# A second Strassen level over pairs of column blocks in the gate/up stage of a gated FNet and GeGLU mix

## The chip, the cores and the metric

One core of one Trainium2 chip runs one program. The metric is the device time of that program in microseconds, as the median of several runs. A profiled execution of the kernel before and its trace are at hand. Engines: PE (TensorE, matmuls), PEld (its weight loads), DVE (VectorE), ACT (ScalarE), POOL (GpSimd, which here only issues stores), SP (SyncE, which only issues loads).

## The reference

For x of 2048 tokens by 640 channels, in float32, the kernel computes

```
g = sigmoid(sum(x * gate_w))                      # one value per token
a = Re(DFT over tokens(DFT over channels(x)))     # four DFT matrices given as inputs
b = (gelu(x @ w_gate) * (x @ w_up)) @ w_down      # w_gate, w_up: 640 x 1728, w_down: 1728 x 640
out = g * a + (1 - g) * b
```

The part that changes is `x @ w_gate` and `x @ w_up`. `gate_w` enters only through g, which is called the gate logit before its sigmoid.

## The kernel before, in words

**Products.** Every float32 product is done in three matmuls (`mm3`, lines 85 to 87): each operand is split into a rounded high part (ACT, `high`, L74) and the rest as low part (DVE, `low`, L77), and high x high, high x low and low x high are added in one PSUM bank. All three have a 128 x 128 weight tile and 512 moving columns.

**Strassen, first level.** Tokens come in four tiles of 512, as two token pairs (`tp` 0 and 1); x is transposed, so that tokens are columns. The 640 channels are five inner blocks of 128. A weight block f holds 128 columns of w_gate and 128 of w_up, so that with two tokens of a pair there is a 2 x 2 block product. Four of the five inner blocks go in two twos, written W[name, i] for i = 0, 1, and are multiplied by Winograd's form of Strassen's scheme with seven products (A11, S1, S2, A12, S3, S4, A22 against B11, T1, T2, B21, T3, B22, T4); the fifth inner block is multiplied plainly (`g5`, `u5` and their difference `D`) and added into the same banks. One block costs 54 matmuls per token pair.

**Order.** The program has five stages one behind the other: a first block of columns (`first_products`), the gate/up stage (`gate_up`, f from 1 to 12), the down product (`split_k`, `step_k`), the Fourier stage over tokens (`cseq`, 64 steps with operands split two steps ahead) and the last product over channels, with the mixing. In the gate/up stage the two token pairs are recorded alternately, step by step, and the order of the instructions on each engine is left to the framework's scheduler; elsewhere `in_order` (L92) fixes the recorded order of the engines that it names. Buffers in SBUF come from pools: `slot` (L64, 48 buffers of 4 KB per partition) for nearly all large tiles, `mtile` (12 of 2 KB), `wsmall` (4 of 1 KB). PSUM has eight banks. A tile's first writer waits until the former owner of its buffer is done.

**Around the change.**

- `load_w` (L186) loads the weights of block f + 1, makes the sums S1 to S4 on DVE and splits both.
- `gate_up` (L259): bank X takes A11, is copied to `s1` (L131), takes S2 on top, is copied to `s2`, then S3 and A22; bank Z takes S1 and `u5`, is copied to `s5` (L277), then S4 and D; bank V takes A12 and `g5`, added to `s1` (L284). Gelu on `s1` (L285) and `s2` (L293). Products and their differences are stored by POOL to DRAM as hA and hT (`keep`, L235), for the down stage.
- After every block come, on DVE, the sums of w_down's (`sum_wd`) or, for the last stage, of the Fourier matrices' blocks (`sum_wu`, L333), each stored in one DMA by `sums_left` (L316).
- `load_z` (L369) loads 128 tokens of x, multiplies by gate_w (L373) and reduces (L374); sixteen times in the stage. `gate_rows` (L350) takes the sigmoid, transposes it on PE (L354) and stores it, after block 10.

Of the kernel before, what the change touches and what calls it, by code (L numbers as in the profile page):

```python
# [1 line left out]

# [22 lines left out]
GM_AT = [2, 15]  # L25
EORD = [0, 2, 1, 3, 4]


@with_exitstack
def kernel(  # L30
# [33 lines left out]
    def slot(dt, shape, name):  # L64
        return pool.tile(shape, dt, tag="s4", name=name, bufs=48)

# [6 lines left out]
    def high(hi, raw):  # L73
        nc.scalar.activation(hi, raw, AF.Copy)  # L74
# [32 lines left out]
    z = pool.tile([P, NS], F32, tag="z", name="z")  # L107
    gwb = slot(F32, [P, D], "gwb")

# [9 lines left out]
    def pair(dt, name):  # L119
        return slot(dt, [P, 2, T], name)  # L120
# [62 lines left out]
    def wsmall(dt, name):  # L183
        return pool.tile([P, 2, P], dt, tag="w", name=name, bufs=4)

    def load_w(f):  # L186
        ra, *a = wchunk(f"wa{f}")
        rb, d = wsmall(F32, f"wb{f}"), wsmall(F32R, f"wd{f}")
        nc.sync.dma_start(ra, wf[f - 1, :, :8])
        nc.sync.dma_start(rb, wf[f - 1, :, 8:])  # L190
        sm, *c = wchunk(f"ws{f}")
        g01, g23, u23 = ra[:, 0:2], ra[:, 2:4], ra[:, 5:7]
        high(a[0], ra)
        tt(sm[:, 0:2], rb, u23, op=ALU.add)
        tt(sm[:, 4:6], g01, rb, op=ALU.subtract)
        tt(sm[:, 2:4], sm[:, 0:2], g01, op=ALU.subtract)
        tt(sm[:, 6:8], g23, sm[:, 2:4], op=ALU.subtract)
        high(c[0], sm)
        low(*a, ra)
        tt(rb[:, 1], ra[:, 4], ra[:, 7], op=ALU.subtract)  # L200
        high(d[:, 0], rb[:, 1])
        low(*c, sm)
        low(d[:, 0], d[:, 1], rb[:, 1])
        W = {"D": (d[:, 0], d[:, 1])}
        for i in range(2):
            W["A11", i], W["A12", i], W["A22", i] = at(a, i), at(a, 2 + i), at(a, 5 + i)
            for k in range(4):
                W[f"S{k + 1}", i] = at(c, 2 * k + i)
        W["g5"], W["u5"] = at(a, 4), at(a, 7)
        return W  # L210

# [44 lines left out]

    hid = {}

    def gate_up(f, W, B, tp, s5):  # L259

        n = f"{f}_{tp}"
        X, Z, V = bank(f"pX{n}"), bank(f"pZ{n}"), bank(f"pV{n}")
# [11 lines left out]
        mm3(Z, W["u5"], x2, False, True)  # L276
        nc.scalar.activation(s5, Z, AF.Copy)  # L277
        yield
        prod(X, "S2", "T2", False)
        s2 = copy(X, f"s2{n}")  # L280
        yield
        prod(V, "A12", (2, 1), True)
        mm3(V, W["g5"], x1, False, True)
        tt(s1, s1, V, op=ALU.add)  # L284
        nc.scalar.activation(s1, s1, AF.Gelu_apprx_tanh)  # L285
        yield
        prod(X, "S3", "T3", False)
        tt(s5, s5, X, op=ALU.add)
        yield
        prod(Z, "S4", (2, 2), False)  # L290
        mm3(Z, W["D"], x2, False, True)
        tt(s2, s2, Z, op=ALU.add)  # L292
        nc.scalar.activation(s2, s2, AF.Gelu_apprx_tanh)  # L293
        tt(s2, s2, s5, op=ALU.mult)  # L294
        keep(hA[tp][k], 1 + 2 * second, s2)
        if second:
            h12, t1 = hid.pop(tp)
            tt(h12, s2, h12, op=ALU.subtract)
# [3 lines left out]
        yield  # L302
        prod(X, "A22", "T4", False)
        mm3(X, W["u5"], x1, False, True)
        tt(s1, s1, X, op=ALU.mult)
        keep(hA[tp][k], 2 * second, s1)
        if second:
            tt(s5, s1, t1, op=ALU.subtract)
            keep(hT[tp][k], 3, s5)
        else:  # L310
            tt(s5, s2, s1, op=ALU.subtract)
            keep(hT[tp][k], 0, s5)
            hid[tp] = s2, s5
        yield

    def sums_left(n, r, a21, to):  # L316

        sm = slot(F32, [P, 8, P], f"{n}s")
        a11, a12, a22 = r[:, 0:2], r[:, 2:4], r[:, 6:8]
        tt(sm[:, 0:2], a21, a22, op=ALU.add)  # L320
        tt(sm[:, 4:6], a11, a21, op=ALU.subtract)
        tt(sm[:, 2:4], sm[:, 0:2], a11, op=ALU.subtract)
        tt(sm[:, 6:8], a12, sm[:, 2:4], op=ALU.subtract)
        nc.gpsimd.dma_start(to, sm)

    def sum_wd(k):

        r, a21 = slot(F32, [P, 8, P], f"dr{k}"), wsmall(F32, f"da{k}")
        nc.sync.dma_start(r, wd[k, :, :8])
        nc.sync.dma_start(a21, wd[k, :, 8:])  # L330
        sums_left(f"d{k}", r, a21, wsd[k])

    def sum_wu(p):  # L333


        r, a21 = slot(F32, [P, 8, P], f"ur{p}"), wsmall(F32, f"ua{p}")
        nc.sync.dma_start(r, wu[p, :, :8])
        nc.sync.dma_start(a21, wu[p, :, 8:])
        if p > 1:
            v, r = r, slot(F32, [P, 8, P], f"un{p}")  # L340
            for a, b in ((0, 2), (2, 4), (4, 5), (5, 8)):
                kept = p == 4 and a in (0, 4)
                nc.scalar.activation(r[:, a:b], v[:, a:b], AF.Copy, scale=1.0 if kept else -1.0)
            if p < 4:
                v, a21 = a21, wsmall(F32, f"ub{p}")
                nc.scalar.activation(a21, v, AF.Copy, scale=-1.0)
            nc.gpsimd.dma_start(wneg[p], r)
        sums_left(f"u{p}", r, a21, wsu[p])

# [18 lines left out]

    def load_z(sb):  # L369

        r = slot(F32, [P, D], f"xz{sb}")
        nc.sync.dma_start(r, xz[sb])
        nc.vector.tensor_tensor(r, r, gwb, op=ALU.mult)  # L373
        nc.vector.tensor_reduce(z[:, sb : sb + 1], r, axis=mybir.AxisListType.X, op=ALU.add)  # L374

# [62 lines left out]
    def load_k(i):  # L438


        tp, b, k = kseq[i]
        n = f"{tp}{b}{k}"
        if k == NK and b:
            return
        r = slot(F32, [P, 8, P], f"kw{n}")
        if k == NK:
            m = slot(F32, [P, 8, P], f"km{n}")
            nc.sync.dma_start(r[:, :5], wd0)
            for q in range(2):
                nc.sync.dma_start(m[q * FR : (q + 1) * FR, :5], wdr)  # L450
            r, src = (r, m), h0[tp]
        elif b:
            nc.sync.dma_start(r[:, 0:2], wd[k, :, 6:8])
            nc.sync.dma_start(r[:, 2:8], wsd[k][:, 0:6])
            src = hT[tp][k]
        else:
            nc.sync.dma_start(r[:, 0:6], wd[k, :, 0:6])
            nc.sync.dma_start(r[:, 6:8], wsd[k][:, 6:8])
            src = hA[tp][k]
        raw = []  # L460
        for q in range(2):
            raw.append(pair(F32, f"kr{n}{q}"))
            nc.sync.dma_start(raw[q], src[:, 2 * q : 2 * q + 2])
        kraw[i] = r, raw

    def split_k(i):
# [160 lines left out]
    with in_order(ACT, DVE, PE):  # L627
# [60 lines left out]
        first_out(bk1, 1, 1)  # L688
        W = load_w(1)
# [4 lines left out]
        tsum(3)  # L694
        his("T1", "T3")
        first_out(bk2, 1, 2)
        lows("T1")
        tsum(2)
        lows("T3")
        his("T2")  # L700
        tsum(4)
        his("T4")
        lows("T2", "T4")
    loads.close()
    Bs.append(B)
    zq = list(range(NS))
    for f in range(1, NF):
        nxt = load_w(f + 1) if f + 1 < NF else None
        s5 = pair(F32, f"s5{f}")
        work = [gate_up(f, W, Bs[tp], tp, s5[:, tp]) for tp in range(2)]  # L710
        for step in range(7):
            for w in work:
                next(w)
            if f == NF - 1 and step >= 4:
                load_k(step - 4)
                if step == 6:
                    split_k(0)
        if f % 2:
            sum_wd(f // 2)
        elif f <= 2 * ND:  # L720
            sum_wu(f // 2 - 1)
        if f == NF - 3:
            gate_rows()
        for _ in range(2):
            if f > 1 and zq:
                load_z(zq.pop(0))
        W = nxt
    order = ctx.enter_context(ExitStack())
# [66 lines left out]
    X = Z = V = L = Q = R = Y = None  # L795
    sv = {}
    for i, (j, ri, b, sp) in enumerate(cseq):
# [321 lines left out]
```

## Time and profile before

| | us |
|---|---|
| median of 3 runs | 1030.67 |
| lowest and highest | 1030.64, 1030.9 |
| the profiled execution | 1030.49 |
| its span, first to last instruction | 1028.7 |

The profile's views tell of one execution, with times in us from the first instruction. A row of a group gives line, engine, operation, what is written and read, the number of instructions, then the busy time of all, the mean of one in ns, and the idle time ahead of them with what ended it. A row of the timeline gives start, duration and the instruction. Matmuls overlap, so the distance between starts says more than their durations. The gate/up stage lies at about 46 to 341 us, the down stage behind it until about 511, the Fourier stage until about 903.

### The profile page before, as it was taken

How to read it: one execution, taken by the hardware profiler on the slowest of the kernel's cores; microseconds unless marked ns; L12 is line 12 of the kernel's file. 1: busy time of each engine (PE TensorE's matmuls, PEld its weight loads, DVE VectorE, ACT ScalarE, POOL GpSimd, SP SyncE). 2: the span in 40 equal slices, each digit the busy share in tenths (PEclk: the TensorE clock that was granted, in tenths of full speed). 3: DMA queues.
4: the chain of work that ended last, by engine and by line, in shares of the span. 5: the costliest groups of instructions: out<-in, count | busy, mean ns of one | idle time of the engine just before them, and what ended most of it. 6: DMA issues, size and time to landing. Idle time of an engine off the chain costs nothing.

```text
span 1028.7 us, 12846 instructions
## 1 busy us (share of the span) xinstructions
PE 1024.4 (100%) x4540; PEld 846.7 (82%) x4540; DVE 774.7 (75%) x1048; ACT 451.7 (44%) x579; POOL 132.1 (13%) x237
## 2 busy tenths in 40 slices
PE   9999999999999999999999999999999999999998
PEld 7888888888888888888888888888888888888887
DVE  6987676767653967985898975796678769697794
ACT  5553333343523646655445443343344344365340
POOL 0112121212121200100010011002000200021121
PEclk9999999999999999999999999999999999999999
DMA  7346554746475978968766667557756777896855
GB/s 268 112 155 227 208 180 148 248 155 234 154 253 202 310 272 276 318 228 290 273 206 234 209 226 277 182 194 246 255 180 215 281 268 277 301 340 205 272 130 90
DMA packets 78929, 234.05 MB, mean 228 GB/s; under 512 B 10160, under 2 KB 18896, under 8 KB 78864
## 3 DMA queue, kind: packets, MB, share of 16 engines
q1 hardware_dynamic: 58144, 169.31, 48.8%
q0 software_dynamic: 20432, 63.73, 18.0%
q8 instruction: 35, 0.57, 0.2%
q14 instruction: 30, 0.25, 0.1%
q10 hardware_dynamic: 288, 0.20, 0.1%
HBM read 169.21 MB, written 63.98 MB: 227 GB/s over the span
## 4 chain that ended last, share of the span: by engine, by line
PE 99%; DMA 0%; DVE 0%; SPq 0%; ACT 0%; issue 0%
PE pX L87 8%; PE pX L85 8%; PE pX L86 8%; PE pZ L87 5%; PE pZ L85 5%; PE pZ L86 5%; PE pV L86 3%; PE pV L85 3%; PE pV L87 3%; PE pL L87 3%; PE pL L85 3%; PE pL L86 3%; PE pY L87 1%; PE pR L87 1%; PE pQ L87 1%; PE pY L86 1%
## 5 line engine op out<-in xcount | busy, mean ns | idle before, releaser
L74 ACT ACTIVATE ch<-csa 128x1024 fp32r<-128x1024 f32 x32 | 34.0, 1062 | 88.1 <-DVE csa L419 53.1
L131 ACT ACTIVATE s<-pX 128x512 f32<-128x512 f32 x64 | 37.8, 595 | 75.5 <-PE pX L87 70.6
L74 ACT ACTIVATE ch<-cra 128x1024 fp32r<-128x1024 f32 x32 | 33.8, 1057 | 46.0 <-PE pL L86 21.6
L77 DVE TENSOR_TENSOR cl<-crb,ch 128x1024 fp32r<-128x1024 f32 x32 | 39.1, 1221 | 17.2 <-ACT ch L74 9.9
L284 DVE TENSOR_TENSOR s<-s,pV 128x512 f32<-128x512 f32 x24 | 16.4, 684 | 44.8 <-PE pV L87 36.7
L77 DVE TENSOR_TENSOR cl<-cra,ch 128x1024 fp32r<-128x1024 f32 x32 | 39.1, 1222 | 14.3 <-ACT ch L74 14.0
L86 PE MATMUL pL<-cl,xah 128*128 128x512 f32 x128 | 49.8, 389 | 0.0
L87 PE MATMUL pL<-ch,xal 128*128 128x512 f32 x128 | 49.8, 389 | 0.0
L235 POOL DMA_DIRECT2D hA<-s x48 | 26.0, 542 | 183.2 <-DVE s L294 175.6
L85 PE MATMUL pL<-ch,xah 128*128 128x512 f32 x128 | 49.3, 389 | 0.0
L77 DVE TENSOR_TENSOR cl<-csb,ch 128x1024 fp32r<-128x1024 f32 x32 | 39.1, 1223 | 6.6 <-ACT ch L74 5.1
L74 ACT ACTIVATE ch<-crb 128x1024 fp32r<-128x1024 f32 x32 | 33.8, 1055 | 21.1 <-DVE cl L77 7.8
L77 DVE TENSOR_TENSOR cl<-csa,ch 128x1024 fp32r<-128x1024 f32 x32 | 39.1, 1221 | 4.0 <-ACT ch L74 3.3
L77 DVE TENSOR_TENSOR kl<-kw,kh 128x1024 fp32r<-128x1024 f32 (+1 forms) x26 | 31.4, 1208 | 11.1 <-ACT kh L74 11.1
L74 ACT ACTIVATE ch<-csb 128x1024 fp32r<-128x1024 f32 x32 | 33.9, 1059 | 12.1 <-PE pL L86 6.9
L293 ACT ACTIVATE s<-s 128x512 f32<-128x512 f32 x24 | 15.2, 633 | 37.7 <-DVE s L292 37.7
L285 ACT ACTIVATE s<-s 128x512 f32<-128x512 f32 x24 | 15.1, 630 | 32.1 <-DVE s L284 32.1
L793 POOL DMA_DIRECT2D uA<-s x16 | 8.7, 542 | 160.0 <-DVE s L839 153.3
L74 ACT ACTIVATE kh<-kw 128x1024 fp32r<-128x1024 f32 (+1 forms) x26 | 27.1, 1041 | 3.8 <-issue 3.5
L86 PEld LDWEIGHTS pL<-cl,xah 128*128 128x128 f32 x128 | 24.0, 188 | 5.0
L87 PEld LDWEIGHTS pL<-ch,xal 128*128 128x128 f32 x128 | 24.0, 188 | 5.0
L85 PEld LDWEIGHTS pL<-ch,xah 128*128 128x128 f32 x128 | 24.0, 188 | 5.0
(3579 smaller groups left out, 3352.5 us busy)
## 6 DMA issues: line engine op xcount, KB each, us to landing
cra<-in_ct SPq DMA_DIRECT2D x64, 512.0 KB, 4.0
crb<-in_ct SPq DMA_DIRECT2D x64, 512.0 KB, 4.8
hA<-s POOLq DMA_DIRECT2D x48, 256.0 KB, 4.7
hT<-s POOLq DMA_DIRECT2D x48, 256.0 KB, 5.6
kr<-hA SPq DMA_DIRECT2D x24, 512.0 KB, 6.3
kr<-hT SPq DMA_DIRECT2D x24, 512.0 KB, 6.9
ux<-uA SPq DMA_DIRECT2D x24, 512.0 KB, 6.1
ux<-uT SPq DMA_DIRECT2D x16, 512.0 KB, 6.7
```

What stands on the lines that cost most here:

```text
L74: nc.scalar.activation(hi, raw, AF.Copy)
L77: nc.vector.tensor_tensor(lo, raw, hi.bitcast(F32), op=ALU.subtract)
L85: nc.tensor.matmul(ps, lh, rh, start=first, stop=False, skip_group_check=True)
L86: nc.tensor.matmul(ps, lh, rl, start=False, stop=False, skip_group_check=True)
L87: nc.tensor.matmul(ps, ll, rh, start=False, stop=last, skip_group_check=True)
L131: nc.scalar.activation(m, src, AF.Copy)
L235: nc.gpsimd.dma_start(to[:, i], src)
L284: tt(s1, s1, V, op=ALU.add)
L285: nc.scalar.activation(s1, s1, AF.Gelu_apprx_tanh)
L293: nc.scalar.activation(s2, s2, AF.Gelu_apprx_tanh)
L793: nc.gpsimd.dma_start(to[:, i], src)
```

## The change

Blocks 3 to 12 are taken as five pairs. In a pair, the product A12 B21 is computed once for both blocks and both token pairs by a second Strassen level: its 2 x 2 block matrices are A12's two inner blocks of the two column blocks, against the two inner blocks of B21 of the two token pairs. `together` computes its seven products (11 `mm3` with the fifth inner block's) into three banks H, Z, V and leaves the sums in `s1t`; `gate_up` then adds its A11 product to `s1t`, or has it added, instead of copying it, and has no bank V for paired blocks. The sums of x across the token pairs are made once, in block 2 (`sums_across`); the combinations of A12 in `make_w` (`across`), from a third load `rq`.

In the stage PE, ACT and DVE keep the recorded order. Work that prepares other blocks is put into a list (`fills`) and recorded between the steps in proportion to matmul time (`fill`, `run`). Loads of weights are two blocks ahead.

The gate logit is one DVE instruction with an accumulator, and a second that reads it out. `gate_rows` comes after block 12. The `sum_wu` pieces move to Fourier steps 4, 17, 19, 21 and 36 and the two behind each; `sums_left` works in place and stores in four DMAs. The slot pool has 47 buffers, `wsmall` 6, and `gwb` its own.

```diff
+PAIRED = 3
+WU_AT = [4, 17, 19, 21, 36]
...
     def slot(dt, shape, name):
-        return pool.tile(shape, dt, tag="s4", name=name, bufs=48)
+        return pool.tile(shape, dt, tag="s4", name=name, bufs=47)
...
-    gwb = slot(F32, [P, D], "gwb")
+    gwb = pool.tile([P, D], F32, tag="gwb", name="gwb")
...
-        return pool.tile([P, 2, P], dt, tag="w", name=name, bufs=4)
+        return pool.tile([P, 2, P], dt, tag="w", name=name, bufs=6)
+
+    def pair_of(f):
+        return 0 if f < PAIRED or f >= NF else 2 - (f - PAIRED + 1) % 2
...
+        def across():
+            tt(rq[:, 3], rq[:, 0], rq[:, 1], op=ALU.add)
+            tt(rq[:, 5], ra[:, 0], rq[:, 0], op=ALU.subtract)
+            tt(rq[:, 4], rq[:, 3], ra[:, 0], op=ALU.subtract)
+
+        def across2():
+            tt(rq[:, 6], ra[:, 1], rq[:, 4], op=ALU.subtract)
+            tt(rq[:, 7], g5, rq[:, 2], op=ALU.subtract)
...
+        if kind == 1:
+            work = [(84, sums), (84, across), (56, across2), (0, high_q), (84, sums2), (0, high_a), (56, diff)]
+            work += [(109, low_q), (0, high_c), (122, low_a), (122, low_c)]
+        elif kind == 2:
+            work = [(84, sums), (28, diff_here), (0, high_a), (84, sums2), (0, high_c), (97, low_a), (122, low_c)]
+        else:
+            work = [(84, sums), (0, high_a), (84, sums2), (0, high_c), (122, low_a), (56, diff), (122, low_c)]
+        return W, work
...
+    def together(f, W, Tp, s1, xs):
+        H, Z, V = (bank(f"p{name}{f}t") for name in "HZV")
+        x1 = [at(Bs[tp][5], 0) for tp in range(2)]
+        mm3(H, W["A12", 0], Tp["B11"], True, True)
+        yield 68
+        s1[0, 0] = copy(H, f"s1{f}00")
+        yield
+        mm3(Z, W["S1p"], Tp["T1"], True, False)
+        mm3(Z, W["g5n"], x1[1], False, True)
+        yield 136
+        s1[1, 1] = copy(Z, f"s1{f}11")
+        yield
+        mm3(V, W["A12", 1], Tp["B21"], True, False)
+        mm3(V, W["g5"], x1[0], False, True)
+        yield 136
+        tt(s1[0, 0], s1[0, 0], V, op=ALU.add)
+        yield
+        mm3(H, W["S2p"], Tp["T2"], False, True)
+        yield 68
+        s1[0, 1] = copy(H, f"s1{f}01")
+        yield
+        mm3(H, W["S3p"], Tp["T3"], False, True)
+        yield 68
+        tt(s1[1, 1], s1[1, 1], H, op=ALU.add)
+        yield
+        mm3(Z, W["S4p"], Tp["B22"], False, False)
+        mm3(Z, W["Dp"], x1[1], False, True)
+        yield 136
+        tt(s1[0, 1], s1[0, 1], Z, op=ALU.add)
+        tt(s1[0, 1], s1[0, 1], xs[1], op=ALU.add)
+        yield
+        mm3(H, W["A22p"], Tp["T4"], False, False)
+        mm3(H, W["g5n"], x1[0], False, True)
+        yield 136
+        s1[1, 0] = copy(H, f"s1{f}10")
+        yield
...
         prod(X, "A11", (1, 1), True)
-        s1 = copy(X, f"s1{n}")
+        yield 136
+        if not kind:
+            s1 = copy(X, f"s1{n}")
+        else:
+            s1 = s1t[kind - 1, tp] if (kind, tp) != (1, 1) else None
+            if s1 is not None:
+                tt(s1, s1, X, op=ALU.add)
...
+        todo.extend([(122, last_sums), (61, last_sum)])
...
-        nc.gpsimd.dma_start(to, sm)
+            for i, v in enumerate((a22, a11, a21, a12)):
+                nc.gpsimd.dma_start(to[:, 2 * i : 2 * i + 2], v)
...
-        nc.vector.tensor_tensor(r, r, gwb, op=ALU.mult)
-        nc.vector.tensor_reduce(z[:, sb : sb + 1], r, axis=mybir.AxisListType.X, op=ALU.add)
+            nc.vector.tensor_tensor_reduce(v, v, gwb, 1.0, 0.0, ALU.mult, ALU.add, z[:, sb : sb + 1])
...
+    def fill(ns):
+        state["pe"] += ns
+        some = False
+        while fills and not (some and not fills[0][0]) and state["done"] <= 1.25 * state["all"] * state["pe"] / state["pe_all"]:
+            cost, do = fills.popleft()
+            do()
+            some = True
+            state["done"] += cost
...
+    with in_order(PE, ACT, DVE):
+        for f in range(1, NF):
...
+            work = [gate_up(f, W, Bs[tp], tp, s5[:, tp], s1t, xs) for tp in range(2)]
+            more = together(f, W, Tp, s1t, xs) if kind == 1 else iter(())
+            for _ in range(4):
+                run(more)
+            for step in range(8 if not kind else 7):
+                for tp, w in enumerate(work):
+                    run(w)
+                    if (step, tp) in ((0, 1), (1, 0)):
+                        run(more)
+                        if step == 0:
+                            run(more)
+                if step == 5:
+                    load_w(f + 2)
...
+            if f == NF - 1:
+                gate_rows()
...
+        for p, at_i in enumerate(WU_AT):
+            if i == at_i:
+                wus[p] = sum_wu(p)
+            if at_i <= i < at_i + 3:
+                next(wus[p], None)
```

More of the change, by code (lines that the diff above doesn't have):

```diff
@@ L1 @@
+from collections import deque
 from contextlib import ExitStack, contextmanager
+from functools import partial
 import concourse.bass as bass
@@ L201, in load_w @@
[L201 to L206, printed above, removed]
-            for k in range(4):
-                W[f"S{k + 1}", i] = at(c, 2 * k + i)
-        W["g5"], W["u5"] = at(a, 4), at(a, 7)
-        return W
+        rq = None
+        if pair_of(f) == 1:
+            rq = slot(F32, [P, 8, P], f"wq{f}r")
+            nc.sync.dma_start(rq[:, 0:3], wf[f, :, 0:3])
@@ L255, in first_out, with gate_up @@
         keep(h0[tp], t - 1, g)
[L257 to L259 removed]
+    hid, todo = {}, deque()
+    def together(f, W, Tp, s1, xs):
[34 more added lines that the diff above has]
+        yield
+    def gate_up(f, W, B, tp, s5, s1t, xs):
         n = f"{f}_{tp}"
[L264 removed]
+        kind = pair_of(f)
+        X, Z = bank(f"pX{n}"), bank(f"pZ{n}")
+        xs[tp] = X
         x1, x2 = at(B[5], 0), at(B[5], 1)
@@ L272, in gate_up @@
         prod(X, "A11", (1, 1), True)
-        s1 = copy(X, f"s1{n}")
-        yield
+        yield 136
+        if not kind:
+            s1 = copy(X, f"s1{n}")
+        else:
+            s1 = s1t[kind - 1, tp] if (kind, tp) != (1, 1) else None
+            if s1 is not None:
+                tt(s1, s1, X, op=ALU.add)
+        yield
+        if not kind:
+            V = bank(f"pV{n}")
+            prod(V, "A12", (2, 1), True)
+            mm3(V, W["g5"], x1, False, True)
+            yield 204
+            tt(s1, s1, V, op=ALU.add)
+            yield
         prod(Z, "S1", "T1", True)
         mm3(Z, W["u5"], x2, False, True)
+        yield 204
         nc.scalar.activation(s5, Z, AF.Copy)
+        if not kind:
+            nc.scalar.activation(s1, s1, AF.Gelu_apprx_tanh)
         yield
         prod(X, "S2", "T2", False)
+        yield 136
         s2 = copy(X, f"s2{n}")
+        if kind:
+            s1 = s1t[kind - 1, tp]
+            nc.scalar.activation(s1, s1, AF.Gelu_apprx_tanh)
         yield
[L282 to L285, printed above, removed]
+        mm3(Z, W["D"], x2, False, False)
+        yield 68
         yield
         prod(X, "S3", "T3", False)
+        yield 136
         tt(s5, s5, X, op=ALU.add)
@@ L367, with load_z, load, total @@
     gm = {}
[L369 to L374, printed above, removed]
+    def load_z(n):
+        r, work = {}, []
+        def load():
+            sb = zq.pop(0)
+            r[0] = sb, slot(F32, [P, D], f"xz{sb}")
+            nc.sync.dma_start(r[0][1], xz[sb])
+        def total():
+            sb, v = r.pop(0)
+            nc.vector.tensor_tensor_reduce(v, v, gwb, 1.0, 0.0, ALU.mult, ALU.add, z[:, sb : sb + 1])
+        load()
+        return [[(80, total)] + [(0, load)] * (k < n - 1) for k in range(n)]
     xa, xb = {}, {}
@@ L464, in load_k, with split_pieces, weights, right @@
         kraw[i] = r, raw
+    def split_pieces(i):
+        n = "{}{}{}".format(*kseq[i])
+        r, raw = kraw.pop(i)
+        names = ("A11", "A12", "e5", "S4")
+        assert not kseq[i][1]
+        B, W = [], {}
+        def weights():
+            h, l = slot(F32R, [P, 8, P], f"kh{n}"), slot(F32R, [P, 8, P], f"kl{n}")
+            split(h, l, r)
+            W.update({name: (at((h, l), 2 * q), at((h, l), 2 * q + 1)) for q, name in enumerate(names)})
+        def right(q):
+            v = hl(f"kb{n}{q}")
+            split(*v, raw[q])
+            B.extend([at(v, 0), at(v, 1)])
+        ktile[i] = W, B
+        return [(122, weights), (122, lambda: right(0)), (122, lambda: right(1))]
     def split_k(i):
@@ L688 @@
         first_out(bk1, 1, 1)
-        W = load_w(1)
+        load_w(1)
+        W, work = make_w(1)
+        for _, do in work:
+            do()
+        load_w(2)
         nc.sync.dma_start(gwb, gw.to_broadcast([P, D]))
@@ L706 @@
     zq = list(range(NS))
[L707 to L727, printed above, removed]
+    Tp, t_raw = {}, {}
@@ new lines, in sums_across, with load, sums, sums2 @@
+    def sums_across():
+        raw = {}
+        def load(name, b, d):
+            raw[name] = mtile(F32, f"xp{name}")
+            nc.sync.dma_start(raw[name], xt[b, d])
+        for name, b, d in (("11", 0, 2), ("12", 2, 2), ("22", 2, 3), ("21", 0, 3)):
+            load(name, b, d)
+        def sums():
+            raw["t1"] = mtile(F32, "xpt1")
+            tt(raw["t1"], raw["12"], raw["11"], op=ALU.subtract)
+            tt(raw["12"], raw["22"], raw["12"], op=ALU.subtract)
+        def sums2():
+            tt(raw["22"], raw["22"], raw["t1"], op=ALU.subtract)
+            tt(raw["21"], raw["21"], raw["22"], op=ALU.subtract)
+        def part(k, v, src):
+            return lambda: split(*v, src) or Tp.update({f"T{k}": v})
+        pairs = hl("xpT")
+        Tp.update(B11=at(Bs[0][2, 1], 0), B21=at(Bs[0][2, 1], 1), B22=at(Bs[1][2, 1], 1))
+        def part1():
+            part(1, at(pairs, 0), raw["t1"])()
+        def part3():
+            part(3, (mtile(F32R, "xp3h"), mtile(F32R, "xp3l")), raw["12"])()
+        work = [(138, sums), (69, part1), (138, sums2), (69, part(2, at(pairs, 1), raw["22"])), (69, part3)]
+        return work, [(69, part(4, at(Bs[1][2, 1], 0), raw["21"]))]
@@ new lines, with run @@
+    fills, state = deque(), {}
+    def fill(ns):
[3 more added lines that the diff above has]
+            cost, do = fills.popleft()
+            do()
+            some = True
+            state["done"] += cost
+    def run(steps):
+        ns = next(steps, None)
+        if ns is not None:
+            fill(ns)
+            next(steps)
+    s1t = {}
+    with in_order(PE, ACT, DVE):
+        for f in range(1, NF):
+            kind = pair_of(f)
+            if f == PAIRED:
+                fills.extend(t34)
+            fills.extend(todo)
+            todo.clear()
+            if f == PAIRED - 1:
+                t12, t34 = sums_across()
+                fills.extend(t12)
+            if f + 1 < NF:
+                nxt, work = make_w(f + 1)
+                fills.extend(work)
+            if f >= PAIRED and (kind == 1 or f == NF - 1):
+                fills.extend(sum_wd((f - PAIRED + 1) // 2))
+            if kind == 1:
+                more, zs = list(fills), load_z(4 if f > NF - 3 else 3)
+                fills.clear()
+                for k, v in enumerate(zs):
+                    a, b = (len(more) * i // len(zs) for i in (k, k + 1))
+                    fills.extend(more[a:b] + v)
+            if f == NF - 1:
+                load_k(0)
+                fills.extend(split_pieces(0))
+            state.update(pe=0, done=0, all=sum(c for c, _ in fills), pe_all=2450 if not kind else 2790 if kind == 1 else 2040)
+            s5 = pair(F32, f"s5{f}")
+            xs = {}
+            work = [gate_up(f, W, Bs[tp], tp, s5[:, tp], s1t, xs) for tp in range(2)]
[11 more added lines that the diff above has]
+                    load_w(f + 2)
+                if f == NF - 1 and step > 4:
+                    load_k(step - 4)
+            while fills:
+                fills.popleft()[1]()
+            if f == NF - 1:
+                gate_rows()
+            W = nxt
+        for _, do in todo:
+            do()
```

146 lines of the change are left out of this document (97 added, 49 removed).

## The prediction

> **What bounds the kernel now.** I read the profile's page first: busy time by engine, the slices of the span, the chain that ended last.
>
> ```profile
> span 1028.7 us, 12846 instructions
> PE 1024.4 (100%) x4540; PEld 846.7 (82%) x4540; DVE 774.7 (75%) x1048; ACT 451.7 (44%) x579; POOL 132.1 (13%) x237
> ...
> PEclk9999999999999999999999999999999999999999
> ...
> PE 99%; DMA 0%; DVE 0%; SPq 0%; ACT 0%; issue 0%
> ```
>
> TensorE has work in 1024.4 of 1028.7 us, at full granted clock in every slice, and 99% of the last chain is its own. A busy PE need not be a full PE, so I then looked at where matmuls start (timeline of PE where the first two column blocks meet) and at the windows by stage.
>
> ```profile
> 62.11 0.39 PE L85 MATMUL pX<-x011h,wa2h 128*128 128x512 f32 x1
> 62.34 0.39 PE L86 MATMUL pX<-x011l,wa2h 128*128 128x512 f32 x1
> ...
> 63.02 0.46 PE L85 MATMUL pZ<-xT01h,ws2h 128*128 128x512 f32 x1
> 63.35 0.50 PE L87 MATMUL pX<-x011h,wa2l 128*128 128x512 f32 x1
> 63.69 0.39 PE L85 MATMUL pX<-x011h,wa2h 128*128 128x512 f32 x1
> 63.92 0.39 PE L85 MATMUL pZ<-x022h,ws1h 128*128 128x512 f32 x1
> ```
>
> ```profile
> core 0: us, PE busy (x) PEld busy (x) DVE busy (x) ACT busy (x) POOL busy (x), PEclk, DMA share, GB/s
> 54.00:343.00 289.00, 289.00 (x1272) 238.13 (x1271) 195.23 (x336) 110.86 (x177) 58.35 (x108) 1.00 0.58 200
> 520.00:890.00 370.00, 370.00 (x1634) 306.35 (x1634) 290.08 (x351) 160.64 (x179) 34.68 (x64) 1.00 0.67 232
> ```
>
> A matmul starts every 0.23 us although each lasts 0.39: they overlap, and the step between starts is the price. Two steps of 0.33 and 0.34 at 63.0 are the only pause in this excerpt, 0.21 us over the normal step. In the gate/up stage (54 to 343 us) 1272 starts take 289 us: 0.2272 us each. The list of waits has hardly anything for PE:
>
> ```profile
> PE idle L631 <- PEq L1107: 0.8, 1, 0.8
> PE pm L86 <- DVE x012l L77: 0.2, 1, 0.2
> ```
>
> So the end moves by 0.227 us for each matmul that goes, and for each moment in which PE must wait.
>
> **The change part by part.**
>
> *Matmuls.* A12 B21 cost, per pair of column blocks and both token pairs, 4 times 2 products of three matmuls plus 4 of the fifth inner block: 36. The second level has seven products, of which four carry an extra product for that inner block: 11 times 3 = 33. Five pairs save 15, and the instruction order of the changed program as built has 4525 matmuls against 4540. Nothing runs beside PE here that could take the gain: 15 x 0.2272 = **-3.41 us**.
>
> *Fixed order in the stage.* The pause at 63.0 stood where the scheduler ran a matmul of block 2 ahead of its weights. In the new order W2 is complete some 6 us before block 2 begins, by the same addition as below: **-0.21**. But now PE, ACT and DVE can't pass a late instruction, so I set the work of each engine against PE's time, block by block, with these rows:
>
> ```profile
> L284 DVE TENSOR_TENSOR s<-s,pV 128x512 f32<-128x512 f32 x24 | 16.4, 684 | 44.8 <-PE pV L87 36.7 <-issue 8.0
> ...
> L373 DVE TENSOR_TENSOR xz<-xz,gwb 128x640 f32<-128x640 f32 x16 | 13.1, 819 | 12.7 <-DMA xz<-in_xz 12.7
> L374 DVE TENSOR_REDUCE z<-xz 128x1 f32<-128x640 f32 x16 | 13.0, 812 | 0.1
> ...
> L77 DVE TENSOR_TENSOR ws9l<-ws9r,ws9h 128x1024 fp32r<-128x1024 f32 x1 | 1.2, 1219 | 0.0
> ...
> L194 DVE TENSOR_TENSOR ws9r<-wb,wa9r 128x256 f32<-128x256 f32 x1 | 0.4, 418 | 0.0
> ...
> L200 DVE TENSOR_TENSOR wb<-wa9r 128x128 f32<-128x128 f32 x1 | 0.3, 282 | 0.0
> ```
>
> ```profile
> L131 ACT ACTIVATE s<-pX 128x512 f32<-128x512 f32 x46 | 27.5, 597 | 56.6 <-PE pX L87 52.2 <-DMA hT<-s 3.6 <-DMA hA<-s 0.8
> ...
> L285 ACT ACTIVATE s<-s 128x512 f32<-128x512 f32 x24 | 15.1, 630 | 32.1 <-DVE s L284 32.1
> ...
> L74 ACT ACTIVATE ws9h<-ws9r 128x1024 fp32r<-128x1024 f32 x1 | 1.1, 1060 | 0.0
> ```
>
> First block of a pair, 123 matmuls, 27.9 us of PE. DVE: 18 ops of 512 columns (12.3), 8 of 256 (3.3), one of 128 (0.3), low parts of 768 and 1024 columns (estimates from the two sizes beside them: 0.9 and 1.2), three fused logits. The fused logit is in no row; its bounds are one pass (0.82, L373) and the two that it replaces plus a short read-out (1.63 + 0.28, L200), and I take 0.9, near the one pass: 2.7. Sum 20.8, 75%. At the upper bound it is 23.7, still under 27.9, and a faster one gains nothing, since PE waits for no logit.
>
> Second block, 90 matmuls, 20.4 us: 10 of 512 (6.8), 4 of 256 (1.7), 7 of 128 (2.0), low parts of 896 and twice 1024 (3.5): 14.0, 69%. The tightest wait there is ACT's, which rounds the next pair's weights between copies that PE waits for. The second Z is summed after 30 matmuls, 6.8 us into the block; then ACT's queue is the copy of Z (to 7.6), 1024 columns rounded (8.7), 128 (9.0), the copy of X (9.6). PE writes that X again after 48 matmuls, at 10.9: 1.3 us to spare.
>
> Block 2, 24.5 us, is fullest: it also makes the T's across the token pairs. DVE has 24 of 512, 4 of 256, 7 of 128 and three long ones: 16.4 + 1.7 + 2.0 + 3.5 = 23.6 us, 96%. Not all of it has to be done inside the block: the last sums wait for its last bank and run on into block 3. The tight place is again ACT: second Z after 48 matmuls (10.9), its copy (11.7), a gelu (12.3), 896 columns rounded (13.3), a copy of X (13.9), 1024 (14.9), 128 (15.2), the other copy of X (15.8); PE wants that bank after 72, at 16.4: 0.5 us. Cost taken: 0, between 0 and 2 us.
>
> *Slots.* The pool goes from 48 to 47 buffers while a pair needs three more (A12's combinations raw, high, low). ACT's rounding of the second block's weights now writes into a buffer that a store to hT must first have left, and behind it on ACT stands the copy of Z that PE waits for.
>
> ```profile
> DMA to landing us min/median/max: 2.5/6.0/8.9
> ```
>
> DVE's sum that releases this store ends 5.7 us into the block. The copy of Z must be done after 78 matmuls (17.7), with another copy and the rounding (0.9) ahead of it: the rounding must start by 15.5, 9.8 us after the store was released. The slowest of 48 stores took 8.9 before. Cost 0, between 0 and what rival C takes.
>
> *End of the stage.* The logits' transpose goes behind the last block, with the sigmoid and its table load ahead of it on ACT:
>
> ```profile
> L352 ACT ACT_TABLE_LOAD x1 | 1.3, 1283 | 0.0
> ...
> L352 ACT ACTIVATE z<-z 128x16 f32<-128x16 f32 x1 | 0.2, 216 | 0.0
> ```
>
> 18 matmuls (4.1 us) cover the chain (a DVE add 0.7, gelu 0.6, table 1.3, sigmoid 0.2, some 0.4 of hand-overs: 3.2). Behind it DVE must finish six last sums (hT) among the low parts of the second down step. Before, the first of these steps had this pause:
>
> ```profile
> 344.80 0.40 PE L85 MATMUL kL<-kb0001h,kh 128*128 128x512 f32 x1
> 345.14 0.50 PE L86 MATMUL kZ<-kb0001l,kh 128*128 128x512 f32 x1
> 345.48 0.39 PE L87 MATMUL kZ<-kb0001h,kl 128*128 128x512 f32 x1
> ```
>
> 0.22 us over two normal steps, 0.25 with a smaller one beside it. In the new order DVE has, from the transpose on, the last product and a small op (1.1), six sums (4.1) and three low parts (3.7): 8.9 us, and PE wants the third low part after 37 matmuls, at 8.4: a pause of about 0.45. **+0.20**, between -0.25 and +1.
>
> *Moved and added work.* The sums for the last stage's weights go into the Fourier stage: 4 x 0.42 = 1.7 us of DVE five times and, three times, four or five short ACT copies of 1024 to 1280 columns together (an estimate of 2 us from L131's row), in steps of 6.8 us with no evacuation. DVE has 290 of 370 us there. What hides them is the lead of the splits, two steps ahead; without it each would cost up to 1.7. The loads there already wait for slots at no cost to PE, and one slot fewer takes part of that lead:
>
> ```profile
> SPq L410 <- PE pL L87: 115.3, 25, 9.3
> ```
>
> Stores in four parts add issues to POOL, which pays for each:
>
> ```profile
> L235 POOL DMA_DIRECT2D hT<-s x48 | 26.0, 542 | 14.1 <-DVE s L298 3.9 <-DVE wd L77 1.9 <-DVE kb0001l L77 1.6
> ```
>
> 33 more are 18 us over the whole span, beside the 58 of 289 that POOL works in the stage; nothing needs these sums before the down and last stages. Cost 0.
>
> *Sum.* The profiled execution took 1030.49 us, 1.8 more than its span, and the median is 0.18 above it. 1030.49 - 3.41 - 0.21 + 0.20 = 1027.07, and on the median's footing **1027.2 us**.
>
> **The rivals.**
>
> *B: the strict order gives half of it back.* If ACT or DVE runs later than added up (0.5 us of margin in block 2, 1.3 in each second block), all matmuls behind wait. For: engines that were free to be reordered by the scheduler no longer are, DVE at 96% in block 2. Against: no wait for DVE or ACT in PE's list above, margins in every block. 0.5 us in each of five pairs: 1029.7. The Trainium skill, "TensorE: Matmul & The Clock Gate" (Part 1, Architectural detail), says that ScalarE and VectorE are strictly first in, first out and that matmuls stay in program order, only weight loads being pulled ahead. By that rule a late copy costs PE its whole lateness, as this rival has it; the trace of before has no late copy to show it.
>
> *C: slower, by the slots.* A store that lands later than 9.8 us holds the rounding, behind it the copy of Z, and PE. Five pairs share one pattern, so it repeats. It decides from a landing of about 10.5 us (5 x 0.7 = 3.5 takes the gain); at 11.3, 5 x 1.5 = 7.5: 1034.7. For: three more buffers in a smaller pool. Against: 8.9 at most before, and less traffic in the stage, since the wu sums leave it. The Trainium skill, "Perfetto Trace Analysis" (Optimization Strategy), reads the same gap repeating on the engine that should be saturated as a sign of too few buffers for the next tile. By that rule the gap would stand at the same place in all five pairs; the trace of before has none.
>
> *D: nothing moves.* That would need another price than the start step; the count of 15 is certain. About 1030.6.
>
> **How the numbers follow.** Forecast 0.75 (1026.6 to 1028.6), B 0.15, C 0.08, D 0.02. 0.2% of 1030.67 is 2.1 us, about what a measurement of this kernel can tell from no change: faster means below 1028.6. Faster 0.75, same 0.17 (B and D), slower 0.08. The range is the forecast's own, reached out to B: 1026.6 to 1029.8.
>
> **What would show it.** In the changed profile: 4525 matmuls; the gate/up stage shorter by 3 to 4 us at an unchanged start step; 123 and 90 matmuls in 27.9 and 20.4 us; PE's list of waits still nearly empty; Fourier and later stages as long as before. The prediction is wrong if PE waits for a copy s or s5 on ACT (B), if ACT waits for hT before a weight's rounding in every pair (C), if the fused logit takes over 3 us, or if a Fourier step waits for its low part.

## The result, and the profile after

| | before | after |
|---|---|---|
| median of 7 runs, us | 1030.66 | 1027.46 |
| lowest and highest | 1030.29, 1030.9 | 1027.04, 1028.46 |
| the profiled execution, us | 1030.49 | 1027.04 |
| its span | 1028.7 | 1025.3 |

The ratio is 0.997, with a 95% interval of 0.9958 to 0.9981. The forecast was 1027.2. The total agrees to 0.3 us, but the terms of the sum do not, and the experiments are about that.

The page of the changed kernel, the rows that answer to those of before:

```profile
span 1025.3 us, 12981 instructions
PE 1020.5 (100%) x4525; PEld 844.2 (82%) x4525; DVE 792.0 (77%) x1096; ACT 448.2 (44%) x580; POOL 149.8 (15%) x270
...
PE 96%; issue 2%; DMA 1%; POOL 0%; DVE 0%; POOLq 0%; DVEq 0%
```

TensorE still bounds the kernel, with 15 matmuls fewer. But its share of the last chain is 96% where it was 99%: something else stands in the chain now. The list of PE's waits names it:

```profile
PE idle L824 <- PEq L1394: 0.8, 1, 0.8
PE pX L89 <- ACT s L135: 0.4, 1, 0.4
PE pR L89 <- DVE s L1126: 0.3, 1, 0.3
```

The two waits below the first are new: PE waits once for a copy by ACT and once for an addition by DVE. The windows by stage tell where. First two rows of before (gate/up, Fourier), then two of the changed kernel:

```profile
45.80:340.90 295.10, 295.10 (x1298) 243.19 (x1297) 199.68 (x340) 113.61 (x182) 57.51 (x107) 1.00 0.58 197
510.80:902.40 391.60, 391.60 (x1729) 324.28 (x1728) 302.52 (x369) 166.54 (x188) 34.68 (x64) 1.00 0.68 238
```

```profile
45.40:336.30 290.90, 290.90 (x1282) 240.39 (x1281) 209.73 (x367) 105.94 (x168) 61.79 (x115) 1.00 0.51 176
506.00:899.00 393.00, 392.23 (x1729) 324.13 (x1728) 311.23 (x390) 169.44 (x200) 47.03 (x87) 1.00 0.74 255
```

The gate/up stage is 4.2 us shorter, more than forecast, and the Fourier stage 1.4 us longer, where the forecast was nothing. With each stage taken from its first matmul to the next stage's first one (timeline of PE; "spread" and "no pairs" are experiments below):

| us | before | after | no pairs | spread |
|---|---|---|---|---|
| start and first columns | 45.79 | 45.40 | 45.48 | 45.78 |
| gate/up | 295.11 | 290.95 | 294.35 | 290.95 |
| down | 169.86 | 169.67 | 169.71 | 169.67 |
| Fourier | 391.68 | 393.05 | 393.55 | 391.68 |
| last product, end | 126.28 | 126.19 | 126.03 | 126.20 |
| span | 1028.73 | 1025.27 | 1029.11 | 1024.28 |

The start differs from run to run (45.4 to 46.9 over all profiles here; 45.78 and 46.17 in two profiles of the spread kernel), and PE waits there for operands split from the first loads; it is not counted to the change.

Where the Fourier stage lost its time, in the timeline of PE of the changed kernel:

```profile
658.11 0.39 PE L91 MATMUL pL<-ch,xal 128*128 128x512 f32 x1
658.92 0.50 PE L89 MATMUL pX<-ch,xbh 128*128 128x512 f32 x1 [0.42 <-ACT s L135]
659.26 0.40 PE L90 MATMUL pX<-cl,xbh 128*128 128x512 f32 x1
...
662.23 0.39 PE L91 MATMUL pR<-ch,xbl 128*128 128x512 f32 x1
662.96 0.50 PE L89 MATMUL pR<-ch,xbh 128*128 128x512 f32 x1 [0.35 <-DVE s L1126]
663.30 0.39 PE L90 MATMUL pR<-cl,xbh 128*128 128x512 f32 x1
```

Two steps of 0.81 and 0.73 us, each with a step of 0.34 behind it, where 0.227 is normal: 1.3 us over. This is the start of step 24, where a group of eight steps ends and its eight banks are read out by ACT and DVE. ACT's timeline before it shows why the copies came late:

```profile
651.24 1.06 ACT L78 ACTIVATE ch<-csa 128x1024 fp32r<-128x1024 f32 x1 [9.92 <-DMA wsu<-ur]
652.21 1.04 ACT L78 ACTIVATE ch<-csb 128x1024 fp32r<-128x1024 f32 x1
653.16 1.32 ACT L504 ACTIVATE ur<-ur 128x256 f32<-128x256 f32 x4
...
655.99 1.06 ACT L78 ACTIVATE ch<-csa 128x1024 fp32r<-128x1024 f32 x1 [1.20 <-issue]
657.33 1.06 ACT L78 ACTIVATE ch<-csb 128x1024 fp32r<-128x1024 f32 x1 [0.27 <-DVE csb L594]
658.29 1.06 ACT L135 ACTIVATE s<-pX 128x512 f32<-128x512 f32 x2
```

For 9.92 us ACT does nothing. The rounding of step 24's matrix block (`ch`) writes into the buffer in which one of the moved sums (`ur`) stood, and that one is free only when its store to DRAM (`wsu<-ur`) has landed. The next rounding, the negation of the next sum (L504) and the copy of bank X (L135) follow in the fixed order. DVE's timeline shows the second half:

```profile
660.51 0.42 DVE L476 TENSOR_TENSOR ur<-ua,ur 128x256 f32<-128x256 f32 x1 [0.81 <-DMA wneg<-ur]
...
661.88 0.42 DVE L481 TENSOR_TENSOR ur<-ur 128x256 f32<-128x256 f32 x1
662.23 1.28 DVE L1126 TENSOR_TENSOR s<-s,pV 128x512 f32<-128x512 f32 x2
```

The next sum works in place, so it waits until its negated copy has been stored (`wneg<-ur`), and the addition for which PE waits stands behind it.

### The profile page after: what moved, and what is told of

Same layout as the page of the kernel before. It is cut to its first block, busy times and chain, and to the rows that moved or that the text cites. A ratio compares the mean times of both kernels' runs of the same rounds, so it can differ in the third digit from the quotient of the medians.

```text
span 1025.3 us, 12981 instructions
## 1 busy us (share of the span) xinstructions
PE 1020.5 (100%) x4525; PEld 844.2 (82%) x4525; DVE 792.0 (77%) x1096; ACT 448.2 (44%) x580; POOL 149.8 (15%) x270
## 4 chain that ended last, share of the span: by engine, by line
PE 96%; issue 2%; DMA 1%; POOL 0%; DVE 0%; POOLq 0%; DVEq 0%
PE pX L91 7%; PE pX L89 7%; PE pX L90 7%; PE pZ L91 4%; PE pZ L89 4%; PE pZ L90 4%; PE pL L91 2%; PE pL L89 2%; PE pL L90 2%; PE pV L91 1%; PE pV L89 1%; PE pV L90 1%; PE pR L89 1%; PE pY L91 1%; PE pY L89 1%
## 5 line engine op out<-in xcount | busy, mean ns | idle before, releaser
L420 ACT ACTIVATE s<-pZ 128x512 f32<-128x512 f32 x24 | 14.3, 597 | 82.8 <-PE pZ L91 82.8
L441 ACT ACTIVATE s<-s 128x512 f32<-128x512 f32 x24 | 15.2, 633 | 61.9 <-DVE s L440 61.9
L135 ACT ACTIVATE s<-pX 128x512 f32<-128x512 f32 x44 | 25.5, 592 | 21.8 <-PE pX L91 21.5
L725 POOL DMA_DIRECT2D out<-ks x12 | 6.5, 540 | 164.9 <-DVE ks L724 164.3
L321 POOL DMA_DIRECT2D hT<-s x48 | 26.0, 541 | 21.8 <-DVE s L464 8.2
```

The source lines that it names most:

```text
L135: nc.scalar.activation(m, src, AF.Copy)
L321: nc.gpsimd.dma_start(to[:, i], src)
L725: nc.gpsimd.dma_start(acc4[:, t] if tp and e == 4 else out[2 * tp + t, e], src)
```

## The experiments

**Theory:** a matmul is worth one start step of 0.227 us, and the Fourier stage's 1.3 us come from one buffer that a slow store holds. **Rivals:** the fixed order made the gain; the moved sums cost their work, wherever they stand.

### No second level

```diff
-        return 0 if f < PAIRED or f >= NF else 2 - (f - PAIRED + 1) % 2
+        return 0
```

The sums across the token pairs go too; everything else of the change stays.

> The changed kernel without the second level: all blocks take A12 B21 plainly, 4540 matmuls again; the fixed order, the fills, the fused logit and the moved sums for the last stage stay. If the 15 matmuls are the gain, at one start step each: 3.4 us above the changed kernel's 1027.46, so 1030.9, with a Fourier stage of 393 us as in the changed kernel. If the fixed order and the moved work made most of the gain, it stays under 1029.

Measured: 1030.9 us, ratio to before 1.0003 (0.9994 to 1.0012). The gate/up stage takes 294.35, 3.40 more than with pairs: 15 x 0.2267. The Fourier stage takes 393.55, so its pauses have nothing to do with the second level. Without the pairs the rest of the change gains 0.77 us in the gate/up stage and loses 1.87 in the Fourier stage.

### The sums at other Fourier steps

```diff
-WU_AT = [4, 17, 19, 21, 36]
+WU_AT = [4, 21, 17, 33, 36]
```

> The changed kernel with the sums for the last stage's weights at Fourier steps 4, 21, 17, 33, 36 instead of 4, 17, 19, 21, 36, so that the two with a negation and an extra store no longer stand close before the end of a group of eight steps. Theory: the 1.33 us that PE stands at 658 to 663 come from a buffer that ACT's rounding can take only when the store wsu<-ur has landed (ACT idle 9.9 us there), so they go: 1026.1, Fourier stage 391.7. Rival: it is the work itself of the moved sums, on DVE and ACT, that delays the copies wherever it stands: 1027.4 again, with the pause elsewhere.

Measured: 1026.29 us (1025.5 to 1026.59), ratio 0.9957 (0.9945 to 0.997), better than both kernels. Its list of PE's waits and its Fourier stage:

```profile
PE idle L824 <- PEq L1394: 0.8, 1, 0.8
```

```profile
506.40:898.10 391.70, 391.70 (x1730) 324.45 (x1729) 311.31 (x390) 170.10 (x200) 47.24 (x87) 1.00 0.74 256
```

DVE does the same 311.3 us of work and ACT the same 170 as in the changed kernel, and PE has no pause. The work itself costs nothing; the rival falls.

### One sum moved

```diff
-WU_AT = [4, 17, 19, 21, 36]
+WU_AT = [4, 17, 33, 21, 36]
```

> The changed kernel with one of the five sums for the last stage moved: the third from Fourier step 19 to 33; the fourth stays at 21. Theory: the third one's buffer is the root (the rounding of step 24 waits for its store, and the negation of the fourth, its store and its sums are late only behind that): both pauses go, 1026.2, Fourier stage 391.7. Rival: the fourth one's own store and sums stand between the additions that PE waits for, whatever came before: the second pause stays, 0.6 to 1.2 us, so 1026.8 to 1027.4.

Measured: 1026.37 us, ratio 0.9959 (0.9947 to 0.9972), Fourier stage 391.68, no wait of PE. The third sum's buffer was the root. The fourth still stands at step 21, but its negated copy landed at 656.9 here, 2 us before PE began step 24, and not 2.1 us after the time at which it could have.

Three kernels hold the sums at the old steps and put a size on it: by the trace, the fourth sum's negated copy landed 2.14, 2.43 and 2.65 us after step 24 could have begun (the changed kernel, two logit instructions, no pairs), and PE's pauses came to 1.3, 1.6 and 1.8 us. A store that lands 0.25 us later costs 0.25 us.

### The sums back in the gate/up stage

```diff
+            if kind == 2:
+                wu_p = sum_wu((f - PAIRED - 1) // 2)
+                next(wu_p)
+                fills.extend([(0, partial(next, wu_p, None)), (168, partial(next, wu_p, None))])
...
-        for p, at_i in enumerate(WU_AT):
-            if i == at_i:
-                wus[p] = sum_wu(p)
-            if at_i <= i < at_i + 3:
-                next(wus[p], None)
```

> The changed kernel with the sums for the last stage's weights back in the gate/up stage, one in the second block of each pair, as fills in the recorded order. Theory: the Fourier stage is then as before the change (391.7 us) and the gate/up stage has room for 1.7 us of DVE in a block of which DVE fills 69%: 1026.1. Rival: the gate/up stage is tight in buffers and on ACT, and the sums cost there what they cost in the Fourier stage, 0.3 us or more in each of five pairs: 1027.4 or more.

Measured: 1043.24 us, ratio 1.0129 (1.0115 to 1.0143). The theory missed by far. The rival had named the buffers and left its time open upward, but its price of 0.3 us a pair was far too small. The Fourier stage is 391.68 as expected, but the gate/up stage takes 16.2 us more:

```profile
PE pX L89 <- DVE s L436: 11.3, 4, 2.8
```

Four of the five pairs wait 2.8 us at the same matmul. DVE's timeline in the first of them:

```profile
139.37 1.22 DVE L81 TENSOR_TENSOR wa5l<-wa5r,wa5h 128x1024 fp32r<-128x1024 f32 x1 [6.23 <-PE pZ L90]
140.51 1.22 DVE L81 TENSOR_TENSOR ws5l<-ws5r,ws5h 128x1024 fp32r<-128x1024 f32 x1
141.65 0.68 DVE L436 TENSOR_TENSOR s<-s,pX 128x512 f32<-128x512 f32 x1
```

DVE stands idle for 6.23 us: the low part of the next block's weights has to write into a buffer that PE's own matmuls into Z still read, and the addition L436, which frees bank X for PE, is behind it. In the spread kernel the same low part starts without a wait, and the addition waits for PE and no longer PE for it:

```profile
132.91 1.22 DVE L81 TENSOR_TENSOR wa5l<-wa5r,wa5h 128x1024 fp32r<-128x1024 f32 x1
135.25 0.69 DVE L436 TENSOR_TENSOR s<-s,pX 128x512 f32<-128x512 f32 x1 [1.11 <-PE pX L91]
```

By the trace that is a wait for a buffer and not for work; the next experiment takes the added work away.

### One buffer less

```diff
-        return pool.tile(shape, dt, tag="s4", name=name, bufs=47)
+        return pool.tile(shape, dt, tag="s4", name=name, bufs=46)
```

From the spread kernel; every instruction and its order on each engine stay.

> The kernel with the sums spread (steps 4, 21, 17, 33, 36) and 46 large buffers instead of 47; every instruction and its order on each engine stay the same. Theory: the pause of 2.8 us in the second blocks of four pairs, which came when the sums stood in the gate/up stage, is one of buffers (DVE's low part of the next weights waits 6.2 us for a buffer that PE still reads, and behind it the addition that PE waits for): with one buffer less the same pause comes at the same place, 2.8 us and some slow matmuls behind it in each of four or five pairs, so 1038 to 1044. Rival: the pause was DVE's 1.7 us of added sums and not the buffer: 1026.3 to 1027, without a pause in the gate/up stage.

Measured: 1040.87 us (1038.99 to 1043.01; the profiled execution is the fastest), ratio 1.0106 (1.0091 to 1.0122). The waits of DVE and of PE in this kernel:

```profile
DVE wa7l L81 <- PE pZ L90: 6.2, 1, 6.2
DVE wa9l L81 <- PE pZ L90: 6.2, 1, 6.2
DVE wa11l L81 <- PE pZ L90: 6.2, 1, 6.2
DVE wa5l L81 <- PE pZ L90: 6.2, 1, 6.2
DVE wa3l L81 <- PE pZ L90: 4.4, 1, 4.4
```

```profile
PE pX L89 <- DVE s L436: 8.5, 5, 1.7
PE pX L89 <- ACT s L135: 1.9, 2, 1.0
```

The same 6.2 us of DVE, for the same reason, ahead of the same matmul in the same four pairs; block 2, ahead of the first pair, joins them with 4.4. PE's part is 1.7 us and not 2.8, since one low part of 1.22 less stands ahead of the addition; five blocks lose 2.0 each (gate/up stage 301.04 against 290.95), the Fourier stage another 2.8. The mechanism is confirmed. The size of a pause was over-estimated: the total lies within the forecast because the Fourier stage lost time too, which was not forecast, and because three of the four executions took 1.2 to 4.0 us longer than the profiled one; what those lost beyond it is not shown. 47 buffers are just enough: the forecast's "cost 0" for the slots was right with nothing to spare.

### Two instructions for a logit

```diff
-            nc.vector.tensor_tensor_reduce(v, v, gwb, 1.0, 0.0, ALU.mult, ALU.add, z[:, sb : sb + 1])
+            nc.vector.tensor_tensor(v, v, gwb, op=ALU.mult)
+            nc.vector.tensor_reduce(z[:, sb : sb + 1], v, axis=mybir.AxisListType.X, op=ALU.add)
```

> The changed kernel with the gate logit in two DVE instructions again (multiply, then reduce) instead of the fused one. If DVE has room in the first block of a pair (75% busy), nothing changes: 1027.5, within 0.5. Rival: DVE's order is tight enough that 0.73 us more for each of three or four logits in a block is late for a copy: 0.5 us in each of five pairs, 1030.

Measured: 1027.47 us, against 1027.46; the gate/up stage takes 290.95 in both. The groups of DVE, first in the changed kernel, then in this one:

```profile
L543 DVE CUSTOM_DVE_ANT_0 xz<-xz,gwb 128x640 f32<-128x640 f32 x16 | 13.1, 820 | 0.2 <-DMA xz<-in_xz 0.2
...
L543 DVE DVE_READ_ACCUMULATOR2_ANT z<- 128x1 f32 x16 | 1.3, 83 | 0.0
```

```profile
L544 DVE TENSOR_REDUCE z<-xz 128x1 f32<-128x640 f32 x16 | 13.1, 820 | 0.5
L543 DVE TENSOR_TENSOR xz<-xz,gwb 128x640 f32<-128x640 f32 x16 | 13.1, 820 | 0.5 <-DMA xz<-in_xz 0.5
```

The fused form takes 0.82 + 0.08 = 0.90 us instead of 1.64 and saves nothing, because DVE has room.

### The order left to the scheduler

```diff
-    with in_order(PE, ACT, DVE):
+    with ExitStack():
```

From the spread kernel, in the gate/up stage only.

> The kernel with the sums spread (steps 4, 21, 17, 33, 36), and the order of the gate/up stage left to the scheduler instead of the recorded one. The matmuls keep their order as built; DVE's and ACT's instructions move. If the 0.77 us by which the gate/up stage without pairs came out shorter than before the change is the fixed order's: at most 0.8 us longer, 1026.3 to 1027.1. If the second level only works in the recorded order (copies and rounding share ACT): pauses in the pairs, 1028 or more.

Measured: 1026.59 us, ratio 0.9962 (0.9949 to 0.9974); gate/up stage 290.95 in both. PE's matmuls came out in the same order in this stage, DVE's and ACT's instructions did not. So the fixed order of DVE and ACT gains nothing: the scheduler's is as good. Another order of the matmuls was not tried. The 0.3 us more in the median are within what the start takes from run to run (46.87 us here).

### The slope

```diff
-        return 0 if f < PAIRED or f >= NF else 2 - (f - PAIRED + 1) % 2
+        return 0 if f < 7 or f >= NF else 2 - (f - PAIRED + 1) % 2
```

Three pairs; and, with the sums spread, no pair and five pairs on the same chip.

> The second level in the last three pairs only (blocks 7 to 12), sums spread: 4531 matmuls. If each pair is worth its three start steps: 0.68 x 2 = 1.36 us above the kernel with five pairs, 1027.7. If the first or the last pair is worth another amount (sums across the token pairs, end of the stage), it lies off this line by over 0.4.

> No second level, with the sums spread over Fourier steps 4, 21, 17, 33, 36: 4540 matmuls and, by theory, no pause in the Fourier stage. If the second level is worth 15 start steps and nothing else, this is 3.4 us above the kernel with pairs and the sums spread (1026.3): 1029.7. If pairs cost something else too, the difference is smaller than 3 us.

> The kernel with five pairs and the sums spread once more, as the foot of this comparison: 1026.3 as in its first measurement, 0.4% below the kernel before the change.

Measured: 1029.96 without pairs, 1027.68 with three, 1026.47 with five (ratio to before 0.9959, 0.9946 to 0.9971). The gate/up stages are 294.35, 292.31 and 290.95 us: 0.68 a pair, three start steps, in the last three pairs as in the first two. No list of PE's waits has an entry beyond the start of the program.

## Why the prediction was right, and where it was not

- **Matmuls, -3.41:** -3.40, by the stage with and without pairs. The price of a matmul on a full PE is the step between starts, and nothing beside it took part of it.
- **Fixed order, -0.21:** the rest of the change gained 0.77 us in the gate/up stage. Of this, 0.21 is the pause at 63.0, as forecast; 0.09 stood behind the transpose of the logits, which now comes where the down stage begins; the rest, some 0.04 us a block, lay in steps of 0.23 to 0.24. Why these shrank stays open. Whether the order removed the pause, as the prediction has it, is open too: the loads are also two blocks ahead now, and in no later kernel does PE run a matmul of block 2 ahead of its weights, not even with the order left to the scheduler.
- **Loads on the engines:** blocks of 123 and 90 matmuls took 27.97 and 20.40 us (forecast 27.9 and 20.4), and DVE 20.9 and 13.6 in them (20.8 and 14.0):

```profile
94.40:122.40 28.00, 28.00 (x124) 23.11 (x124) 20.87 (x38) 8.67 (x14) 7.48 (x14) 1.00 0.55 190
122.40:142.80 20.40, 20.40 (x91) 16.90 (x90) 13.63 (x26) 7.49 (x12) 3.37 (x7) 1.00 0.39 137
69.90:94.40 24.50, 24.50 (x109) 20.25 (x108) 18.17 (x33) 10.89 (x18) 3.34 (x7) 1.00 0.31 105
```

 Block 2 (the third row) had 33 instructions in 18.2 us, not the 38 in 23.6 that the prediction added up. No copy was late in this stage, so rival B did not come. Its sign, PE waiting for a copy by ACT, did show once, for 0.42 us, in the Fourier stage.
- **Slots in the stage, 0:** right, and rival C did not come in this stage: the slowest of the 48 stores to hT landed after 8.6 us by the trace (7.8 before), against the 9.8 from which C begins. The view's row for the tile shows more:

```profile
DMA to landing us min/median/max: 2.3/4.9/9.1
```

 The row counts the 24 loads of hT in the down stage with the stores, and its slowest entry is one of these loads. So is the 8.9 of the row before, which the prediction took for the slowest store; the margin of rival C was 2.0 us and not 0.9.

 The sentence on repeating gaps (the Trainium skill, "Perfetto Trace Analysis", Optimization Strategy) fits the two kernels that lacked one buffer: PE's gap of 2.8 or 1.7 us stands at the same matmul of four pairs, with DVE's wait of 6.2 us behind it. It does not say which buffer, and the one that ran out was a weight's low part and not the store's. The pool also shrank less than the prediction took it to: before, `gwb` held one of the 48 buffers until its last use at 255.7 us, and now it has its own, so up to there 47 were left for the other tiles in both kernels.
- **Start of the down stage, +0.20:** it is 0.19 us shorter. The forecast pause of 0.45 at the third low part did not come:

```profile
337.26 0.67 DVE L458 TENSOR_TENSOR s<-s,s 128x512 f32<-128x512 f32 x1
337.86 0.67 DVE L460 TENSOR_TENSOR s<-s,s 128x512 f32<-128x512 f32 x1
338.47 1.21 DVE L81 TENSOR_TENSOR kl<-kw,kh 128x1024 fp32r<-128x1024 f32 x1
339.60 0.67 DVE L464 TENSOR_TENSOR s<-s,s 128x512 f32<-128x512 f32 x1
...
343.14 1.21 DVE L81 TENSOR_TENSOR kb0011l<-kr,kb0011h 128x1024 fp32r<-128x1024 f32 x1
```

 The low part ends at 344.35, PE takes it at 344.86. The sum of durations was 8.9 us in the prediction and is 8.6 with those of this trace; the instructions took 7.8, because one starts 0.60 us behind another that lasts 0.67, and 1.13 behind one of 1.21.
- **Moved work, 0:** the step that failed, +1.37 us. It said that nothing needs these sums before the last stage, and that the lead of the splits hides their work. Both hold, as the spread kernel shows. What is needed is the buffer under them: it was counted as one slot fewer for loads, not as a slot that ACT's next rounding must write into while a store is still reading it.

So the forecast of 1027.2 was met by errors that cancel: 0.56 us too little gain in the stage, 0.39 us too little at the down stage, 0.39 us of a shorter start, and 1.37 us of loss in the Fourier stage that was not seen. That they cancel is luck; the term for the matmuls alone is confirmed by its own experiment. Rival C's mechanism, a store that holds ACT's rounding through a buffer, did come; it was looked for in the stage that the diff is about and stood in another.

## What to carry to other kernels

On a full TensorE the count of matmuls times the start step is the gain, here to 0.01 us. Work moved into a stage with time to spare is priced by its buffers first: ask who takes the buffer next, on which engine it stands, and when the store that frees it lands. A long wait of an engine off the critical path (ACT's 9.9 us, DVE's 6.2) is the place to look when PE's own waits of 0.3 to 0.4 us name only the last link; and a pool that is just large enough shows no wait at all until one buffer less costs 14.6 us (1040.87 against 1026.29).

## What the runs showed of the hardware

Pauses can cost more than their length. In the kernel with the sums in the gate/up stage, matmuls behind the pause of the first pair started 0.43 us apart and not 0.23:

```profile
139.17 0.39 PE L91 MATMUL pZ<-x122h,ws4l 128*128 128x512 f32 x1
142.38 0.50 PE L89 MATMUL pX<-xT04h,wa4h 128*128 128x512 f32 x1 [2.82 <-DVE s L436]
...
143.69 0.63 PE L90 MATMUL pX<-xT04l,wa4h 128*128 128x512 f32 x1
144.12 0.63 PE L91 MATMUL pX<-xT04h,wa4l 128*128 128x512 f32 x1
```

The windows of the same kernel, behind the first pause and behind the second, have the granted clock in the column ahead of the DMA share:

```profile
143.30:146.30 3.00, 3.00 (x9) 2.33 (x8) 2.87 (x6) 1.03 (x2) 1.94 (x4) 0.50 0.88 302
195.80:198.80 3.00, 3.00 (x13) 2.17 (x12) 2.93 (x6) 0.43 (x1) 2.17 (x4) 1.00 0.88 270
```

The clock was halved for about 3 us behind two of the four equal pauses (3.2 us from start to start), which made those blocks 1.3 us longer than the other two, 25.13 against 23.79. How often it happens differs between executions: the other three of this kernel took 0.6 to 3.8 us longer, at a mean granted clock of 0.992 to 0.995 against 0.997 here. Behind the five pauses of 2.1 us with 46 buffers it stayed at 1.00 in the profiled execution; one of the other three, the slowest, had a mean of 0.998. The Trainium skill, "TensorE: Matmul & The Clock Gate" (Part 1), has the clock fall back after an idle window of about 3.4 us that runs freely, and gives 426.7 ns between starts of 512 columns at the low clock. The step of 0.43 agrees; the clock here fell back behind an idle stretch of 2.8 us, shorter than that window, in some places and not in others.
